# A fused attention and feed-forward kernel: attention tiles placed by a table, no warm-up matmuls, an order with a delay per unit, and another ending of the last block

## The chip, the cores and the metric

The kernel runs on one core of a Trainium2 chip. Time is device time in microseconds (us), the median of several executions. A profiled execution stands beside it: the trace has every instruction of the five engines (TensorE, called PE; VectorE, DVE; ScalarE, ACT; GpSimd, POOL; SyncE, SP), the DMA queues, and the clock granted to TensorE.

## The reference

Eight batches, eight heads, 576 tokens, head size 64, all in fp32. A random-feature attention comes first, then a feed-forward layer over all 4608 tokens:

```python
def phi(x):
    proj = np.einsum('bhsd,df->bhsf', x, w_phi)                  # 64 -> 128 features
    proj = proj - np.max(np.abs(proj), axis=-1, keepdims=True)
    return np.concatenate([np.exp(proj), np.exp(-proj)], axis=-1)
q_p, k_p = (phi(q), phi(k))
kv = np.einsum('bhsf,bhsd->bhfd', k_p, v);  z = np.sum(k_p, axis=2)
num = np.einsum('bhsf,bhfd->bhsd', q_p, kv)
den = np.einsum('bhsf,bhf->bhs', q_p, z)[..., None] + 1e-06
x = (num / den), heads side by side, (4608, 512)
h = x @ w_in                                                     # 512 -> 2048
out = (0.5 * h * (1 + erf(h / sqrt(2)))) @ w_out                 # 2048 -> 512
```

## The kernel before

**Attention**, batch by batch. `k_unit` projects 512 keys of two heads into a pair of PSUM banks (`pk`), VectorE takes the maximum of the absolute values and subtracts it, ScalarE makes the two exponentials (`ek`), and 80 small matmuls sum them with the values into `kv`. `q_front` projects queries (`pq`), ScalarE copies them out (`pc`), GpSimd takes the maximum over the partitions (`mb`), VectorE subtracts, ScalarE makes `ef`; then TensorE forms numerators (`pn`) and, in batches 0 to 2, denominators (`dn`). `xo` and `do` are the copies of these, which SP stores to DRAM. `quotients` fetches the denominators, takes reciprocals and stores them. Batch 0 has its queries in two halves; the other batches have a main part of 512 tokens and a rest of 64.

**Weights.** The inputs `w_in` and `w_out` come as 64-bit numbers. `split_weight` loads each of 32 pieces and makes a high and a low fp32r part of it, with five VectorE and two ScalarE instructions. A weight's tile (`w_i0_0` to `w_i3_3`, `w_o0` to `w_o15`) is empty until its raw load.

**The layer** runs over 18 blocks of 256 tokens. `tokens` fetches a block from DRAM, divides, and splits it into `xh` and `xl`. Each of 8 units in a block does two first-layer groups of 12 matmuls into a PSUM tile `ph` (`up`), a gelu on ScalarE, a split of its result, and the second-layer matmuls. Blocks 0 to 7 (`block`) sum in `po`. Blocks 8 to 17 (`seven`) use a seven-product scheme on 2x2 quarters: the products m1 to m7 are summed in `pa0`, `pa1` and `pb`, and at the block's end ScalarE copies four of them into two tiles `ob`, VectorE adds or subtracts the others, and the two tiles are stored. The sums of weights that this needs are made by `sums_of_weights` and kept in DRAM until block 8.

**What sets the order.** The program describes all operations to a planner (`Plan.op`), each with its engine, an assumed cost, the buffers that it reads and writes, and a rank. `Plan.order` then goes through a model of the engines: at each step the operation that can start first goes, and among those of an engine that can start together the lowest rank. A buffer has a tag with so many slots (`Plan.pool`); an operation that needs a slot waits in the model until one is free, and within a stream (`k`, `q`, `f`, `w`, ...) the buffers of a tag are taken in the order in which they were described. The order that comes out is emitted, and every engine's queue executes it strictly. TensorE leaves the layer's matmuls for attention work only if `LUMP` us of that work is ready or some of it has waited `LINGER` us. `PULL`, `URGE`, `BIAS` (for a change of ScalarE's table), `HOLD` (batch 1 not before), `WPACE` (a weight not before) and `SUMSAT`, `SUMSEACH` are further constants of the planner. Four matmuls on a tile of zeros (`WARM`, tile `spin`) open TensorE's queue.

`mm` is the helper at line 342 that issues every matmul, so that all matmuls have this line; `tt` (L383) and `copy` (L377) are the helpers of most VectorE and ScalarE instructions. L395 is the raw load of a weight, L475, L477 and L542 are the loads of keys, values and queries, L558 is the store of `xo`, L848 that of the last block.

Of the kernel before, what the change touches and what calls it, by code (L numbers as in the profile page):

```python
# [27 lines left out]
P = 128  # L28
# [13 lines left out]
class Buf:  # L42


    def __init__(self, plan, tag, make):
        self.plan, self.tag, self.make = plan, tag, make
# [12 lines left out]
class Op:  # L59
    __slots__ = ("eng", "cost", "fn", "bufs", "rank", "table", "late", "deps", "users", "wait", "ready", "start", "end", "n", "names", "nbytes", "duty", "kind", "port", "part", "reopen")  # L60


class Plan:
# [15 lines left out]
    def __init__(self, tc):  # L79
        self.banks = ("ph", "po", "pp", "kv", "pn")  # L80
        self.tc, self.ops, self.slots, self.lines, self.stream, self.since = tc, [], {}, {}, None, 0.0

# [188 lines left out]
def mm_cost(m, n):  # L271
    return n * 0.443 / 1e3
# [27 lines left out]
def fused_kernel(ctx: ExitStack, tc: tile.TileContext, qT, kT, va, w_st, w_in, w_out, out):  # L300
# [25 lines left out]
    def turn_over():  # L326
# [10 lines left out]
    ps = {t: plan.pool(ppool, t, n) for t, n in dict(ph=2, po=1).items()} | {  # L337
        t: plan.pool(lambda: shared[1], t, n) for t, n in dict(pp=1, kv=1, pn=1, pa0=1, pa1=1, h0=1, h1=1).items()}
    op = plan.op

# [48 lines left out]
    def split_weight(src, nm, rank):  # L389
        tag = f"w_{nm}"  # L390
        raw = plan.pool(spool, tag, 1)([P, 512, 2], U32, f"raw_{nm}")
# [63 lines left out]
    def k_rest(b, rank):  # L455
        k = lambda: dict(rank=next(rank))
        plan.stream = "k"
        kr = sb["kr"]([P, 2, P], F32, f"kr_{b}")
# [7 lines left out]
    def k_quad(b, g, kvs, rank, rest):  # L466
# [5 lines left out]
        kts, vts = [], []  # L472
        for p in range(2):
            kt = (early(4 * g + p) if b == 0 else sb["kt"])([P, 4 * P], F32, f"kt_{nm}_{p}")
            op("sp", 0.06, lambda kt=kt, p=p: nc.sync.dma_start(out=kt(), in_=kT[b, g, :, 4 * P * p : 4 * P * (p + 1)]), w=[kt], kb=262, **k())  # L475
# [3 lines left out]
            vts.append(vt)  # L479
        for p in range(2):  # L480
            kt, vt = kts[p], vts[p]
            e = [sb[EARLY_EK[p] if b == 0 else "ek"]([P, 2, 4, NF], F32, f"ek_{nm}_{p}_{s}") for s in (1, 0)][::-1]
# [50 lines left out]
    def q_pair(b, p, kvs, rank, halves=(0, 1)):  # L533
# [4 lines left out]
        for half in halves:  # L538
            nm = f"{b}_{p}_{half}"
            at, n = PIECES[b][half]  # L540
            main = "" if n == HS else " main"
# [45 lines left out]
    def q_rest(b, kvs, rank):  # L587
        k = lambda x=0: dict(rank=next(rank))
        plan.stream = "q"
        nm, n = f"{b}_rest", 4 * HR  # L590
# [46 lines left out]
    def quotients(b, half, rank):  # L637
        plan.stream = "r"
        nm = f"{b}_{half}"
# [30 lines left out]
    def tokens(j, rank):  # L670
        plan.stream = "f"
        xr = sb["xr"]([P, NCC, TB], F32, f"xr_{j}")
# [45 lines left out]
    def block(j, rank):  # L718
        x = tokens(j, rank)
        po = ps["po"]([P, 2, DM], F32, f"po_{j}")  # L720
        for u in range(NU):
            rk = rank(u / NU)
            ph = ps["ph"]([P, 2, TB], F32, f"ph_{j}_{u}")
            up(j, u, (2 * u, 2 * u + 1), ph, x, rk)
# [5 lines left out]
            for i in range(2):  # L730
# [12 lines left out]

                op("pe", 6 * mm_cost(128, DM), mm2, r=[gh, gl, wo[2 * u + i]], w=[po], rank=rk)
        for m in range(2):
            ob = sb["ob"]([P, DM], F32, f"ob_{j}_{m}")
# [6 lines left out]
    def sums_of_weights(rank):  # L753
# [3 lines left out]
        for k in range(NFC // 2):  # L757
# [3 lines left out]
            for i, (x, xc, y, yc, o) in enumerate((  # L761
                    (b, low_cols, a, high_cols, ALU.add), (b, low_cols, b, high_cols, ALU.add), (a, low_cols, a, high_cols, ALU.add),
                    (b, high_cols, a, high_cols, ALU.subtract), (a, low_cols, b, low_cols, ALU.subtract))):
                kw = dict(rank=rank(n / 40))
                plan.since = SUMSAT + SUMSEACH * n
                n += 1
# [10 lines left out]
    def fetch_sums(stored, rank, after):  # L777
        plan.stream = "t"
        tw = []
        for k in range(NFC // 2):  # L780
            kw = dict(rank=rank(k / 8) - 20)
            a, b, d = wo[k], wo[k + 8], stored[k]
            t = sb[f"tw{k}"]([P, 3, 2, HDM], F32R, f"tw_{k}")
# [6 lines left out]
    def seven(j, tw, rank, after):  # L790
# [4 lines left out]
        part = dict(m4=lambda: pa0()[:, left], m5=lambda: pa0()[:, right], m3=lambda: pa1()[:, left], m2=lambda: pa1()[:, right],  # L795
                    m7=lambda: pb()[:, 0, left], m6=lambda: pb()[:, 0, right], m1=lambda: pb()[:, 1, left])
        for u in range(NU):
            rk = rank(u / NU)
            ph = ph_all = ps["ph" if u % 4 < 2 else f"h{u % 2}"]([P, 2, TB], F32, f"ph_{j}_{u}")
            late = after if u < 4 else ()  # L800
            up(j, u, (u, u + 8), ph, x, rk, late if u > 1 else ())
            dr = dict(rank=URGE + rk)
# [22 lines left out]
                     ("m1", uh, ul, 2, lambda i, t=tw[u]: t()[:, 0, 1 - i]))  # L825
            for group, acc in ((terms[:2], pa0), (terms[2:4], pa1), (terms[4:6], pb), (terms[6:], pb)):

                def products(group=group, u=u):
                    ins = []
                    for m, h, l, n, w in group:  # L830
                        for g, i in ((h, 0), (h, 1), (l, 0)):
                            k = len(ins) % 3
                            ins.append(mm(part[m](), lhsT=g()[:, n], rhs=w(i), start=u == 0 and k == 0 and m in ("m4", "m3", "m7", "m1"),
                                          stop=u == NU - 1 and k == 2 and m in ("m5", "m2", "m6", "m1"), skip_group_check=True))
                    return ins

                op("pe", 3 * len(group) * mm_cost(128, HDM), products, r=[group[0][1], group[0][2], a, b, tw[u]], w=[acc], rank=rk)
# [3 lines left out]
        for c, m, x, acc in ((c11, 0, "m4", pa0), (c12, 0, "m5", pa0), (c21, 1, "m2", pa1), (c22, 1, "m3", pa1)):  # L841
            copy("act", act(HDM, True), c, part[x], [acc], [tops[m]], **kw)
        for c, m, x, acc, o in ((c11, 0, "m5", pa0, ALU.subtract), (c12, 0, "m3", pa1, ALU.add), (c21, 1, "m4", pa0, ALU.add), (c22, 1, "m2", pa1, ALU.subtract),
                                (c11, 0, "m7", pb, ALU.subtract), (c22, 1, "m6", pb, ALU.add), (c11, 0, "m1", pb, ALU.add), (c22, 1, "m1", pb, ALU.add)):
            tt("dve", dve(HDM, True), c, c, part[x], o, [acc, tops[m]], [tops[m]], port=False, **kw)
        for m in range(2):
            eng = "act" if j == NBLK - 1 and m else "sp"
            op(eng, 0.06, lambda m=m, eng=eng: (nc.scalar if eng == "act" else nc.sync).dma_start(  # L848
                out=out[j * TB + m * P : j * TB + (m + 1) * P, :], in_=tops[m]()), r=[tops[m]], kb=262, rank=rank(1))

# [32 lines left out]


SEVEN = 8
SUMS = 2
SUMSAT = 190.75
SUMSEACH = 4.989
SUMSPAN = 581.86
T15 = 870.02  # L890
T18 = 997.68
BIAS = 151.84
STICK = 2
PATIENCE = 4.09
URGE = -1000.0
EARLY = 41.32
WPACE = 4.81
# [11 lines left out]
HOLD = 32.35  # L909
WR = -23.78  # L910
# [3 lines left out]
POOLSLACK = 0.3  # L914
DMASLACK = 0.23
T0 = 85.1
# [43 lines left out]
```

## Time and profile before

| | |
|---|---|
| median of 3 runs | 1060.81 us (1060.12 to 1062.88) |
| profiled execution | 1061.28 us, span 1059.1 us |
| TensorE busy | 1028.1 us, 97% |
| VectorE busy | 680.2 us, 64% |
| ScalarE busy | 614.6 us, 58% |
| GpSimd busy | 276.6 us, 26% |
| mean granted clock of TensorE | 0.989 |

The span is from the first to the last instruction. Busy shares are means over stages that differ: attention and weights until about 200 us, the layer with attention in between until about 615 us, the layer alone after that. The ends of matmuls are modelled, so that a busy TensorE is not one at its peak; the steps between the starts of matmuls say more.

### The profile page before, as it was taken

Reading aid. Unit: us, or ns where it says so; the run is one execution under the profiler, and the core shown is the slowest. Engines: PE = TensorE matmul, PEld = TensorE weight load, DVE = VectorE, ACT = ScalarE, POOL = GpSimd, SP = SyncE. Lnnn points to the kernel's source line nnn. Section 1 sums busy time; section 2 is a strip of 40 time slices with the busy share of each in tenths; the row PEclk is TensorE's granted clock in tenths of the full one; section 3 lists DMA queues with packets and bytes.
Section 4 is the critical chain, followed back from the end, with each engine's and each line's share of the span. In section 5 each row is a group of like instructions: output and inputs, shape, how many; then the busy total and the mean of one; then the engine's idle time right before and its main releaser. Section 6 shows DMA issues by size and latency. Waiting matters only on the chain.

```text
span 1059.1 us, 24222 instructions
## 1 busy us (share of the span) xinstructions
PE 1028.1 (97%) x10083; PEld 897.7 (85%) x10083; DVE 680.2 (64%) x1209; ACT 614.6 (58%) x1007; POOL 276.6 (26%) x72
## 2 busy tenths in 40 slices
PE   6778999999999999999999999999999999999997
PEld 4555677778877778887887899999999999999997
DVE  4989999788797897256454333556465565565464
ACT  4878899778776668776465523334444344344343
POOL 2134221454255565565656310000000000000000
PEclk7989999999999999999999999999999999999999
DMA  7587672433535334124121166111111021021000
GB/s 263 153 256 220 198 224 77 132 126 123 153 119 160 104 125 149 56 75 127 34 75 42 60 235 224 41 41 41 41 41 41 21 61 37 24 61 29 14 21 20
DMA packets 87037, 107.10 MB, mean 101 GB/s; under 512 B 28988, under 2 KB 56700, under 8 KB 86928
## 3 DMA queue, kind: packets, MB, share of 16 engines
q1 hardware_dynamic: 86784, 105.30, 32.4%
q8 instruction: 79, 1.29, 0.5%
q14 instruction: 30, 0.25, 0.1%
q10 hardware_dynamic: 144, 0.26, 0.1%
HBM read 75.87 MB, written 29.66 MB: 100 GB/s over the span
## 4 chain that ended last, share of the span: by engine, by line
PE 83%; ACT 6%; DVE 6%; DMA 3%; issue 2%; SPq 0%; ACTq 0%; DVEq 0%
PE ph L342 34%; PE po L342 14%; PE pa L342 10%; PE pb L342 8%; PE kv L342 6%; PE pn L342 4%; PE pk L342 3%; PE pq L342 2%; DMA x_d<-xo 2%; DVE ts L383 1%; ACT ek L452 1%; ACT ef L524 1%; DMA t_d<-ts 1%; ACT L727 1%; DMA vt<-in_va_dram 1%
## 5 line engine op out<-in xcount | busy, mean ns | idle before, releaser
L342 PE MATMUL ph<-xh,w_i 128*128 128x256 f32 x2304 | 414.3, 278 | 0.0
L342 PEld LDWEIGHTS ph<-xh,w_i 128*128 128x128 f32 x2304 | 355.7, 188 | 8.9 <-issue 7.2
L342 PE MATMUL ph<-xl,w_i 128*128 128x256 f32 x1152 | 318.6, 277 | 0.0
L342 PEld LDWEIGHTS ph<-xl,w_i 128*128 128x128 f32 x1152 | 216.3, 188 | 0.2
L383 DVE TENSOR_TENSOR sg<-ga 128x256 f32<-128x256 f32 (+1 forms) x240 | 84.2, 376 | 155.3 <-ACT ga L804 147.7
L519 POOL PARTITION_ALL_REDUCE mb<-pc x36 | 122.2, 3395 | 169.4 <-ACT pc L377 138.4
L342 PE MATMUL po<-w_o,gh 128*128 128x512 f32 (+1 forms) x517 | 163.3, 398 | 0.0
L804 ACT ACTIVATE ga<-ph 128x512 f32<-128x512 f32 x80 | 48.0, 600 | 174.3 <-PE ph L342 172.5
L530 POOL PARTITION_ALL_REDUCE db<-pc x20 | 124.2, 6208 | 83.1 <-DVE pc L579 83.1
L342 PEld LDWEIGHTS po<-w_o,gh 128*128 128x128 f32 x517 | 93.2, 188 | 31.6 <-issue 5.2
L342 PE MATMUL pa<-w_o,oh 128*128 128x256 f32 x640 | 112.9, 276 | 0.0
L342 PE MATMUL po<-w_o,gl 128*128 128x512 f32 (+1 forms) x282 | 101.1, 373 | 1.2 <-DVE gl L383 1.2
L342 PEld LDWEIGHTS pa<-w_o,oh 128*128 128x128 f32 x640 | 96.4, 188 | 0.0
L383 DVE TENSOR_TENSOR gl<-ph,gh 128x512 fp32r<-128x512 f32 x64 | 44.0, 688 | 77.0 <-ACT ph L728 76.4
L342 PE MATMUL pa<-w_o,ol 128*128 128x256 f32 x320 | 88.3, 276 | 0.0
L342 PE MATMUL pb<-tw,uh 128*128 128x256 f32 x480 | 85.6, 276 | 0.0
L727 ACT ACTIVATE gh<-ph 128x512 fp32r<-128x512 f32 x64 | 38.3, 598 | 63.5 <-PE ph L342 63.0
L524 ACT ACTIVATE ef<-pc 128x1024 f32<-128x1024 f32 (+1 forms) x72 | 67.3, 972 | 11.1 <-DVE pc L383 10.9
L342 PEld LDWEIGHTS pb<-tw,uh 128*128 128x128 f32 x480 | 72.3, 188 | 0.0
L452 ACT ACTIVATE ek<-ek 128x1024 f32<-128x1024 f32 x64 | 67.6, 1058 | 6.9 <-DVE ek L383 6.2
L342 PE MATMUL kv<-vt,ek 128*64 128x65 f32 x2048 | 67.5, 225 | 0.0
L342 PE MATMUL pb<-tw,ul 128*128 128x256 f32 x240 | 66.3, 276 | 0.0
(90 smaller groups left out, 1596.2 us busy)
## 6 DMA issues: line engine op xcount, KB each, us to landing
vt<-in_va_dram SPq DMA_DIRECT2D x32, 325.0 KB
t_d<-ts SPq DMA_DIRECT2D x40, 256.0 KB
out_dram<-ob SPq DMA_DIRECT2D x35, 256.0 KB
kt<-in_kT_dram SPq DMA_DIRECT2D x32, 256.0 KB
raw_i<-in_w_in_dram SPq DMA_DIRECT2D x16, 512.0 KB
raw_o<-in_w_out_dram SPq DMA_DIRECT2D x16, 512.0 KB
qt<-in_qT_dram SPq DMA_DIRECT2D x28, 256.0 KB
x_d<-xo SPq DMA_DIRECT2D x28, 256.0 KB
```

What stands on the lines that cost most here:

```text
L342: return tc.keep_in_program_order(nc.tensor.matmul(*a, **kw))
L383: op(eng, cost, lambda: e.tensor_tensor(out=dst(), in0=a(), in1=b(), op=o), r=r, w=w, **kw)
L452: op("act", act(256 * n), lambda s=s: nc.scalar.activation(e[s](), e[1](), AF.Exp, scale=1.0 - 2.0 * s), r=[e[1]], w=[e[s]], table="exp", ...
L519: op("pool", plan.SPENT[most], lambda: nc.gpsimd.partition_all_reduce(mb(), pc(), P, bass_isa.ReduceOp.absmax), r=[pc], w=[mb], port=most, ...
L524: op("act", act(2 * n), lambda s=s: nc.scalar.activation(ef[s](), pc(), AF.Exp, scale=1.0 - 2.0 * s), r=[pc], w=[ef[s]], table="exp", **k())
L530: op("pool", plan.SPENT[total], lambda: nc.gpsimd.partition_all_reduce(db(), pc()[:, :2], P, bass_isa.ReduceOp.add), r=[pc], w=[db], port= ...
L727: op("act", act(2 * TB, True) + 0.016, lambda gh=gh, ph=ph: nc.scalar.activation(gh(), ph(), AF.Gelu), r=[ph], w=[gh], table="gelu", rank= ...
L804: op("act", act(2 * TB, True) + 0.037, lambda ph=ph, ga=ga: nc.scalar.activation(ga(), ph(), AF.Gelu), r=[ph_all], w=[ga], table="gelu", a ...
```

## The change

1. `Plan.pool` looks a tile's name up in a table `HOME`. Where it stands there, the tile takes a slot of the tag that the table gives and not of its own. The table has 210 tiles of batches 0 to 2: SBUF tiles go to the weights' tiles (`w_i0_2` to `w_i3_3`, `w_o8` to `w_o15`) or to other tags' slots (`xh`, `xl`, `gh`, `gl`, `ef`, `ek`, `pc`, `mb`, `db`); PSUM tiles go from `pp`, `kv` and `pn` to `po`, `ph` and each other.
2. `WARM` is 0: the four matmuls on zeros are gone.
3. Every operation belongs to a unit (`plan.unit`: a weight, half a pair of heads, a unit of a block, ...), and a table `DELAY` adds a number of its own to the ranks of each of 360 units. Constants of the planner change: `BIAS` 151.84 to 551.516, `PATIENCE` 4.09 to 2.138, `LUMP` 2.69 to 82.289, `LINGER` 4.65 to 6.494, `HOLD` 32.35 to 23.07, `WPACE` 4.81 to 4.989, `SUMSAT` 190.75 to 175.933, `SUMSEACH` 4.989 to 3.384, `DMASLACK` 0.23 to 0.517.
4. In the last block the product m6 has a bank of its own (`pc`, in the slot of `h1`); the first-layer groups rank 2.2 units earlier and use three slots; the products m1, m7 and m6 of the last two units come after all others, in this order; dependencies are kept by product and by quarter of the output and not by bank and tile; and the four quarters are stored one by one, 128 KB each, from SP's and ScalarE's queues in turn.

```diff
     def pool(self, pool, tag, bufs):
         self.slots[tag] = bufs
-        return lambda shape, dt, name: Buf(self, tag, lambda: (pool() if callable(pool) else pool).tile(shape, dt, tag=tag, name=name, bufs=bufs))
+        self.pools[tag] = pool
+        def new(shape, dt, name):
+            home = HOME.get(name, tag)
+            def make():
+                pool = self.pools[home]
+                return (pool() if callable(pool) else pool).tile(shape, dt, tag=home, name=name, bufs=self.slots[home])
+            b = Buf(self, home, make, name)
+            return b
...
+        o.unit = self.unit
+        o.rank += DELAY.get(self.unit, 0.0)
...
+        last = j == NBLK - 1
+        if last:
+            pc = ps["h1"]([P, DM], F32, f"pc_{j}")
+            part["m6"] = lambda: pc()[:, left]
...
-            up(j, u, (u, u + 8), ph, x, rk, late if u > 1 else ())
+            up(j, u, (u, u + 8), ph, x, rank((u - 2.2) / NU) if last else rk, late if u > 1 else ())
...
+            groups = [(u, terms[:2]), (u, terms[2:4])]
+            if last and u >= NU - 2:
+                put_off += [(x, u, terms[x : x + 1]) for x in (4, 5, 6)]
+            else:
+                groups += [(u, terms[4:6]), (u, terms[6:])]
+            if u == NU - 1:
+                groups += [(v, group) for x in (6, 4, 5) for y, v, group in put_off if x == y]
...
+        final = ((c11, 0, 0, "m7", ALU.subtract), (c22, 1, 1, "m6", ALU.add)), ((c11, 0, 0, "m1", ALU.add), (c22, 1, 1, "m1", ALU.add))
...
+        if last:
+            for m, h, eng in ((0, 1, "sp"), (1, 0, "act"), (0, 0, "sp"), (1, 1, "act")):
+                op(eng, 0.06, lambda m=m, h=h, eng=eng: (nc.scalar if eng == "act" else nc.sync).dma_start(
+                    out=out[j * TB + m * P : j * TB + (m + 1) * P, h * HDM : (h + 1) * HDM], in_=tops[m]()[:, h * HDM : (h + 1) * HDM]),
+                   r=[halves[m, h]], also=[tops[m]], kb=131, rank=rank(1))
+            return
...
+DELAY = {
+    "start": -1266.9, "k0r": -1919.4, "k00": -1383.5, "k01": -1239, "k02": -1008.7, "k03": -1069.9, "q000": -1527.1, "q010": -1691.4, "q020": -1252.1,
...
+HOME = {
+    "kr_0": "w_i2_3", "pk_0_r": "po", "mx_0_r": "gl", "er_0_1": "w_o10", "er_0_0": "xl", "kt_0_0_0": "ef", "vt_0_0_0": "w_i1_2", "kt_0_0_1": "xh",
...
-WARM = 4
+WARM = 0
...
-LUMP = 2.69
-LINGER = 4.65
+LUMP = 82.289
+LINGER = 6.494
```

## Rows read from the trace of the kernel before

**Rows 1.** The page: the span, and each engine's busy time, share and instructions.

```profile
span 1059.1 us, 24222 instructions
PE 1028.1 (97%) x10083; PEld 897.7 (85%) x10083; DVE 680.2 (64%) x1209; ACT 614.6 (58%) x1007; POOL 276.6 (26%) x72
```

**Rows 2.** Stretches: length, busy time of PE, PEld, DVE, ACT, POOL, granted clock, DMA.

```profile
0.00:40.00 40.00, 30.62 (x454) 23.08 (x454) 26.34 (x38) 22.68 (x35) 6.80 (x7) 0.83 0.63 217
40.00:80.00 40.00, 29.98 (x484) 21.03 (x488) 34.38 (x49) 30.31 (x56) 15.10 (x6) 0.91 0.81 229
...
360.00:400.00 40.00, 37.70 (x332) 29.98 (x332) 36.67 (x54) 27.00 (x42) 21.18 (x6) 1.00 0.38 122
...
680.00:720.00 40.00, 40.00 (x355) 40.00 (x354) 24.50 (x64) 17.60 (x39) 0.00 (x0) 1.00 0.13 41
```

**Rows 3.** The same view, the first 10 and 90 us and the 70 us after.

```profile
0.00:10.00 10.00, 6.66 (x16) 2.68 (x16) 0.48 (x1) 2.42 (x4) 1.24 (x5) 1.00 0.78 248
...
0.00:90.00 90.00, 67.88 (x1034) 47.37 (x1036) 70.68 (x97) 61.49 (x102) 25.75 (x14) 0.89 0.71 221
90.00:160.00 70.00, 69.64 (x830) 49.61 (x827) 63.92 (x102) 62.52 (x91) 22.61 (x7) 1.00 0.71 213
```

**Rows 4.** Timeline of the start: start, us, engine, line, operation, tiles, count [idle before].

```profile
1.17 0.89 SPq L542 DMA_DIRECT2D qt<-in_qT_dram  x2
...
2.27 5.22 PE L342 MATMUL spin<-idle 128*128 128x512 f32 x8 [2.27 <-ACT idle L364]
...
7.41 0.76 PE L342 MATMUL pq<-qt,wst 64*128 64x288 f32 x4
...
18.46 1.33 PE L342 MATMUL pq<-qt,wst 64*128 64x288 f32 x4 [1.46 <-issue]
```

**Rows 5.** Chain of waits until 120 us: start, us, what.

```profile
41.15 4.64 DMA x_d<-xo
...
58.19 4.41 DMA x_d<-xo
```

**Rows 6.** Waits from 20 to 80 us: us in total, times, longest.

```profile
PE pk L342 <- ACT pc L377: 5.2, 5, 1.5
ACT xo L377 <- DMA x_d<-xo: 3.1, 3, 1.4
```

**Rows 7.** Waits of SP's queue from 20 to 80 us.

```profile
SPq L558 <- ACT xo L377: 12.6, 4, 10.0
```

**Rows 8.** Timeline of the end, and one stretch of it.

```profile
1053.47 0.28 PE L342 MATMUL pb<-tw,ul 128*128 128x256 f32 x1
...
1054.77 1.20 DVE L383 TENSOR_TENSOR ob<-ob,pb 128x256 f32<-128x256 f32 x3
...
1056.00 0.37 ACTq L848 DMA_DIRECT2D out_dram<-ob  x1
...
1057.00:1058.00 1.00, 0.00 (x0) 0.00 (x0) 0.00 (x0) 0.00 (x0) 0.00 (x0) 0.50 0.59 221
```

**Rows 9.** Timeline of weight loads at the start, and the stretch from 13 to 25 us.

```profile
4.13 0.34 PEld L342 LDWEIGHTS spin<-idle 128*128 128x128 f32 x1 [0.52 <-issue]
...
6.03 0.19 PEld L342 LDWEIGHTS spin<-idle 128*128 128x128 f32 x1 [0.24 <-issue]
...
13.00:25.00 12.00, 9.59 (x98) 8.31 (x100) 9.74 (x12) 8.41 (x12) 4.16 (x2) 0.50 0.65 239
```

**Rows 10.** Timeline of TensorE around the first and the last change to attention work.

```profile
94.04 0.28 PE L342 MATMUL ph<-xh,w_i 128*128 128x256 f32 x1
94.25 1.94 PE L342 MATMUL pn<-ef,kvn 128*64 128x512 f32 x8
...
613.51 0.28 PE L342 MATMUL ph<-xl,w_i 128*128 128x256 f32 x1
613.62 0.28 PE L342 MATMUL ph<-xh,w_i 128*128 128x256 f32 x1
613.83 1.15 PE L342 MATMUL pn_rest<-ef_rest,kvn 128*64 128x64 f32 x32
```

More of the change, by code (lines that the diff above doesn't have):

```diff
@@ L59 @@
 class Op:
-    __slots__ = ("eng", "cost", "fn", "bufs", "rank", "table", "late", "deps", "users", "wait", "ready", "start", "end", "n", "names", "nbytes", "duty", "kind", "port", "part", "reopen")
+    __slots__ = ("eng", "cost", "fn", "bufs", "rank", "table", "late", "deps", "users", "wait", "ready", "start", "end", "n", "names", "nbytes", "duty", "kind", "port", "part", "reopen", "unit")
 class Plan:
@@ L80, in __init__ @@
         self.banks = ("ph", "po", "pp", "kv", "pn")
-        self.tc, self.ops, self.slots, self.lines, self.stream, self.since = tc, [], {}, {}, None, 0.0
+        self.pools = {}
+        self.tc, self.ops, self.slots, self.lines, self.stream, self.since, self.unit = tc, [], {}, {}, None, 0.0, "start"
     def turn(self, a, b):
@@ L338, in fused_kernel @@
         t: plan.pool(lambda: shared[1], t, n) for t, n in dict(pp=1, kv=1, pn=1, pa0=1, pa1=1, h0=1, h1=1).items()}
+    for tag in [f"w_o{f}" for f in range(NFC)] + [f"w_i{c}_{q}" for c in range(NCC) for q in range(4)]:
+        plan.pool(spool, tag, 1)
     op = plan.op
@@ L389, in split_weight @@
     def split_weight(src, nm, rank):
-        tag = f"w_{nm}"
+        tag = plan.unit = f"w_{nm}"
         raw = plan.pool(spool, tag, 1)([P, 512, 2], U32, f"raw_{nm}")
@@ L456, in k_rest @@
         k = lambda: dict(rank=next(rank))
-        plan.stream = "k"
+        plan.stream, plan.unit = "k", f"k{b}r"
         kr = sb["kr"]([P, 2, P], F32, f"kr_{b}")
@@ L473, in k_quad @@
         for p in range(2):
+            plan.unit = f"k{b}{2 * g + p}"
             kt = (early(4 * g + p) if b == 0 else sb["kt"])([P, 4 * P], F32, f"kt_{nm}_{p}")
@@ L480, in k_quad @@
         for p in range(2):
+            plan.unit = f"k{b}{2 * g + p}"
             kt, vt = kts[p], vts[p]
@@ L539, in q_pair @@
             nm = f"{b}_{p}_{half}"
+            plan.unit = f"q{b}{p}{half}"
             at, n = PIECES[b][half]
@@ L588, in q_rest @@
         k = lambda x=0: dict(rank=next(rank))
-        plan.stream = "q"
+        plan.stream, plan.unit = "q", f"q{b}r"
         nm, n = f"{b}_rest", 4 * HR
@@ L637, in quotients @@
     def quotients(b, half, rank):
-        plan.stream = "r"
+        plan.stream, plan.unit = "r", f"r{b}{half}"
         nm = f"{b}_{half}"
@@ L670, in tokens @@
     def tokens(j, rank):
-        plan.stream = "f"
+        plan.stream, plan.unit = "f", f"t{j}"
         xr = sb["xr"]([P, NCC, TB], F32, f"xr_{j}")
@@ L722, in block @@
             rk = rank(u / NU)
+            plan.unit = f"b{j}_{u}"
             ph = ps["ph"]([P, 2, TB], F32, f"ph_{j}_{u}")
@@ L744, in block @@
                 op("pe", 6 * mm_cost(128, DM), mm2, r=[gh, gl, wo[2 * u + i]], w=[po], rank=rk)
+        plan.unit = f"o{j}"
         for m in range(2):
@@ L764, in sums_of_weights @@
                 kw = dict(rank=rank(n / 40))
+                plan.unit = f"s{n}"
                 plan.since = SUMSAT + SUMSEACH * n
@@ L781, in fetch_sums @@
             kw = dict(rank=rank(k / 8) - 20)
+            plan.unit = f"f{k}"
             a, b, d = wo[k], wo[k + 8], stored[k]
@@ L796, in seven @@
                     m7=lambda: pb()[:, 0, left], m6=lambda: pb()[:, 0, right], m1=lambda: pb()[:, 1, left])
+        last = j == NBLK - 1
+        if last:
+            pc = ps["h1"]([P, DM], F32, f"pc_{j}")
+            part["m6"] = lambda: pc()[:, left]
+        own = {m: Buf(plan, None, None) for m in part}
+        held = dict(m4=pa0, m5=pa0, m3=pa1, m2=pa1, m7=pb, m6=pc if last else pb, m1=pb)
+        put_off = []
+        firsts = ("m4", "m3", "m7", "m1", *(("m6",) if last else ()))
+        stops = ("m5", "m2", "m6", "m1", *(("m7",) if last else ()))
         for u in range(NU):
             rk = rank(u / NU)
-            ph = ph_all = ps["ph" if u % 4 < 2 else f"h{u % 2}"]([P, 2, TB], F32, f"ph_{j}_{u}")
+            plan.unit = f"b{j}_{u}"
+            ph = ph_all = ps[("ph", "ph", "h0")[u % 3] if last else "ph" if u % 4 < 2 else f"h{u % 2}"]([P, 2, TB], F32, f"ph_{j}_{u}")
             late = after if u < 4 else ()
-            up(j, u, (u, u + 8), ph, x, rk, late if u > 1 else ())
+            up(j, u, (u, u + 8), ph, x, rank((u - 2.2) / NU) if last else rk, late if u > 1 else ())
             dr = dict(rank=URGE + rk)
@@ L825, in seven, with products @@
                      ("m1", uh, ul, 2, lambda i, t=tw[u]: t()[:, 0, 1 - i]))
[L826 to L828 removed]
+            groups = [(u, terms[:2]), (u, terms[2:4])]
[5 more added lines that the diff above has]
+                groups += [(v, group) for x in (6, 4, 5) for y, v, group in put_off if x == y]
+            for v, group in groups:
+                def products(group=group, u=v):
                     ins = []
@@ L832, in products @@
                             k = len(ins) % 3
-                            ins.append(mm(part[m](), lhsT=g()[:, n], rhs=w(i), start=u == 0 and k == 0 and m in ("m4", "m3", "m7", "m1"),
-                                          stop=u == NU - 1 and k == 2 and m in ("m5", "m2", "m6", "m1"), skip_group_check=True))
-                    return ins
-                op("pe", 3 * len(group) * mm_cost(128, HDM), products, r=[group[0][1], group[0][2], a, b, tw[u]], w=[acc], rank=rk)
+                            ins.append(mm(part[m](), lhsT=g()[:, n], rhs=w(i), start=u == 0 and k == 0 and m in firsts,
+                                          stop=u == NU - 1 and k == 2 and m in stops, skip_group_check=True))
+                    return ins
+                op("pe", 3 * len(group) * mm_cost(128, HDM), products, r=[group[0][1], group[0][2], wo[v], wo[v + 8], tw[v]],
+                   w=[own[m] for m, *_ in group], also=[held[m] for m, *_ in group], rank=rk)
+        plan.unit = f"o{j}"
         tops = [sb["ob"]([P, DM], F32, f"ob_{j}_{m}") for m in range(2)]
@@ L840, in seven @@
         kw = dict(rank=URGE + rank(1))
[L841 to L845, printed above, removed]
+        halves = {(m, h): Buf(plan, None, None) for m in range(2) for h in range(2)}
@@ new lines, in seven @@
+        for c, m, h, x in ((c11, 0, 0, "m4"), (c12, 0, 1, "m5"), (c21, 1, 0, "m2"), (c22, 1, 1, "m3")):
+            copy("act", act(HDM, True), c, part[x], [own[x]], [halves[m, h]], also=[tops[m], held[x]], **kw)
+        final = ((c11, 0, 0, "m7", ALU.subtract), (c22, 1, 1, "m6", ALU.add)), ((c11, 0, 0, "m1", ALU.add), (c22, 1, 1, "m1", ALU.add))
+        for c, m, h, x, o in ((c11, 0, 0, "m5", ALU.subtract), (c12, 0, 1, "m3", ALU.add), (c21, 1, 0, "m4", ALU.add), (c22, 1, 1, "m2", ALU.subtract),
+                              *final[last], *final[not last]):
+            tt("dve", dve(HDM, True), c, c, part[x], o, [own[x], halves[m, h]], [halves[m, h]], also=[tops[m], held[x]], port=False, **kw)
```

27 lines of the change are left out of this document (15 added, 12 removed), and 69 rows, old and new, of tables (DELAY, HOME).

## The prediction

> **What bounds the kernel now.** I read the busy shares first: TensorE is at 97% of a span of 1059.1 us [rows 1], so only what TensorE does not do in the other 3%, does slowly, or does between two kinds of work can be won. The stretches of 40 us then say where that lies [rows 2]. From 680 us on a stretch is 40.00 of 40 us busy with 355 matmuls, at clock 1.00: nothing to win there except at the very end. In the first two stretches TensorE is busy 30.62 and 29.98 us at a granted clock of 0.83 and 0.91; 360 to 400 us has 2.30 us idle. Over the first 90 us it is 67.88 of 90 busy [rows 3], so 22.1 us are idle, 2.3 of them before the first matmul [rows 4].
>
> What ends the waits there: the chain of waits runs four times through the store of an attention result, `x_d<-xo`, from 41.15 us on; first and last of the four pieces take 4.64 and 4.41 us [rows 5]. ScalarE cannot write the next `xo` until one of its two tiles has been stored. ScalarE itself stands only 3.1 us for it, and TensorE waits 5.2 us, five times, for ScalarE to clear the one bank pair that projections use (`pk` after `pc`) [rows 6]. So the start is a net of few buffers, in which TensorE, ScalarE and SP take turns.
>
> The engine behind it is VectorE: 70.68 of the first 90 us, and 63.92 of the next 70 [rows 3], which is 91%. Once TensorE is full it is VectorE (splitting weights, the attention's maxima and differences) that decides how early the layer can be fed.
>
> The profiled execution took 1061.28 us, 2.2 us more than its span; the median of the runs is 1060.81. I sum against 1061.28 and take off the 0.5 at the end.
>
> **The change part by part.**
>
> *Tiles of batches 0 to 2 by the table.* No instruction is added or removed; the same tiles lie elsewhere, so that `xo`, `do`, `pc`, `ef`, `ek` no longer queue for two tiles of their own, and projections, `kv`, `pn` and `dn` get the layer's `ph` and `po` banks. That removes the store from the chain [rows 5] and most of the 5.2 us [rows 6]. What is late next is VectorE. It cannot start before a projection: its first 10 us hold 0.48 us of work now [rows 3]. Between 10 and 160 us it works 134 of 150 us (70.68 + 63.92 less that start) [rows 3], so the whole slack behind the start is 16 us; it has to do the same work before TensorE can be fed. Upper bound of the gain 16 us, lower bound 0 (VectorE as slack as today). Below nothing is the rival at the end. In 90 to 160 us, with no such queue, VectorE stands at 91%; bringing 10 to 90 us from 70.2/80 = 88% to about 96% shortens that stretch to 73 us. I take 7 us.
>
> The table adds waits too: a weight's raw load cannot be issued until the attention tile that lies in its place has been read. SP is one queue in program order, and behind a waiting load stand all other loads and stores; SP already waits up to 10.0 us in one piece for an `xo` to be written [rows 7]. I take this as hidden by loads issued well ahead; its price without that cover is the last rival.
>
> *No matmuls on zeros.* Four warm-up matmuls (8 passes in the trace) fill TensorE from 2.27 us for 5.22 us, and the first projection follows on their heels at 7.41 [rows 4]. Its input is issued from 1.17 us on [rows 4]. How long such a load takes is not in a row; the nearest is the last store, 3.1 us from issue to the end of the span [rows 8], so the projection could start near 4.5 us: 3 us earlier at best, 0 if the load lands at 7. Against that stands the clock. [...] Net I take 0.5 us gained, bounds 3 gained and 1.7 lost, outside the clock rival below.
>
> [...]
>
> *Order by a delay per unit, and the planner's constants.* All instructions stay; their order on TensorE, ScalarE, VectorE and SP changes over the whole run. Two things can be priced. First, the limits on leaving the layer's matmuls: the planner now waits until a piece of attention work has stood 6.494 us (4.65 before), and no longer until 2.69 us of it are there. Each excursion costs a turn: within a run the step is 0.11 us, into the attention work 0.21 (94.04 to 94.25, and at the last 613.62 to 613.83) [rows 10]. That is 0.1 us more; for the way back I take the same, an estimate, so 0.2 per excursion. I count 63 of them between 94 and 615 us, of which the first and the last stand in the rows: 12.6 us in all. If their number falls as 4.65 to 6.494, to 45, 18 turns go: 3.6 us; I take 3.5. Bounds 0 and 12.6. Second, the idle time of 360 to 400 us [rows 2]: 2.30 us. I take 1 us off, bounds 2.3 gained and 2.3 lost (an order that makes as large a hole elsewhere). The larger cost of a table switch on ScalarE and the earlier sums of weights I put at nothing: they only matter where VectorE and ScalarE are full, which is in the 7 us above; after 400 us TensorE has no idle time that they could fill.
>
> *Last block's ending.* The first-layer matmuls of the last block come 2.2 units earlier, and products m1, m7, m6 of the last two units are put behind the others; the same matmuls at the same step, no DMA moved. Their cover is TensorE's own full queue (40.00 of 40) [rows 2]; without it a gelu chain of some 2 us would show. After the last matmul (ends 1053.47 + 0.28 = 1053.75) VectorE now works until 1055.97, and the second store is issued at 1056.00; the end is 1059.1 [rows 8]: 5.35 us. Afterwards one difference is left: a third of 1.20, 0.40 us, behind some 0.3 us of hand-over, then the store: 0.7 instead of 2.25, 1.5 saved. The store is half as large; data still moved for 0.59 of the microsecond from 1057 [rows 8], so 0.3 of that may go too. I take 1.8, bounds 1.2 and 2.4.
>
> Sum: 7 + 0.5 + 3.5 + 1 + 1.8 = 13.8 us; 1061.3 - 13.8 - 0.5 = **1047**.
>
> **The rivals.**
>
> *VectorE holds the start where it is.* For it: 91% from 90 to 160 us with TensorE full. Against it: 88% before, with waits for `pk` and stores in between. Then 7 us fall away: 1054.
>
> [...]
>
> *Everything priced comes in:* 16 at the start, 2.4 at the end, 5 of turns, 2.3 of holes, 2 from the zeros: 27.7, so 1033. Against it: VectorE would have to work without a gap for 150 us.
>
> *Slower: weights late behind attention tiles.* Place: SP's queue from 60 to 150 us, where the raw loads of the late weights now wait for tiles of batches 1 and 2 to be read. The first layer block cannot finish until every weight is split, and only one block sums at a time, so TensorE falls back on attention work alone, at the rate of the first 80 us: 60.6 of 80 [rows 2], 24% idle. Over 70 us that is 17 us, against which stand the 6.8 us of the other parts: 1061.3 + 17 - 6.8 - 0.5 = 1071. It decides the sign from about 7 us of new idle time. For it: one wait of 10.0 us on SP already [rows 7]. Against it: loads of weights are far fewer than the time for them, and the table covers mostly late weights.
>
> **How the numbers follow.** Forecast 1047: 0.57 (its own range 1040 to 1052). VectorE holds: 0.17. Clock: 0.06. Everything: 0.07. Slower: 0.13. The range 1036 to 1059 leaves out part of the best case and the slower one. A measurement of this kernel tells about 0.3% from no change: 1057.6 to 1064.0. Faster takes nearly all of the first four, 0.80; within takes the edge of "VectorE holds" and a weak form of the slower case, 0.09; slower 0.11.
>
> **What would show it.** Right: no `x_d<-xo` in the chain before 90 us; TensorE's idle time in the first 90 us at about 15 in place of 22 us, VectorE there above 76; fewer than 50 excursions; 3.5 us from the last matmul to the end, with one VectorE instruction between. [...] Slower rival: TensorE below 95% between 80 and 200 us. The prediction is wrong if VectorE's share before 160 us does not rise, or if holes of several us appear after 200 us.

## The result, and the profile after

The changed kernel takes 1047.34 us (median of 4 runs, 1045.0 to 1049.29), the kernel before 1061.85 in the same runs; the ratio is 0.9859, with a 95% interval of 0.9825 to 0.9893. The prediction was 1047. Its total is right, and by place most of its terms come close; what stands behind them is in part something else, and the larger part of this section and the next is about that.

The page of the kernel after: span, busy times, and the shares of the chain of waits by engine.

```profile
span 1046.6 us, 24197 instructions
PE 1019.6 (97%) x10070; PEld 893.1 (85%) x10070; DVE 661.1 (63%) x1209; ACT 614.5 (59%) x1011; POOL 276.9 (26%) x72
PE 90%; DVE 5%; ACT 2%; issue 1%; DMA 1%; SPq 0%; DVEq 0%; ACTq 0%
```

Stretches of it (length, then busy time of PE, PEld, DVE, ACT, POOL, clock, DMA).

```profile
0.00:10.00 10.00, 3.62 (x28) 3.08 (x28) 2.59 (x4) 2.43 (x4) 0.19 (x4) 1.00 0.76 227
...
0.00:40.00 40.00, 27.34 (x504) 21.80 (x504) 29.12 (x38) 26.35 (x45) 9.12 (x8) 0.96 0.77 255
...
0.00:90.00 90.00, 70.38 (x1126) 49.62 (x1127) 72.66 (x98) 65.43 (x109) 30.19 (x15) 0.92 0.73 237
90.00:160.00 70.00, 68.25 (x789) 49.10 (x788) 67.56 (x104) 60.55 (x90) 22.71 (x7) 1.00 0.60 187
160.00:200.00 40.00, 38.73 (x540) 31.51 (x534) 38.39 (x63) 37.03 (x56) 8.07 (x3) 1.00 0.41 117
...
360.00:400.00 40.00, 40.00 (x331) 32.87 (x331) 27.44 (x44) 29.93 (x39) 19.33 (x4) 1.00 0.39 121
...
680.00:720.00 40.00, 40.00 (x355) 40.00 (x355) 19.01 (x54) 14.29 (x33) 0.00 (x0) 1.00 0.05 16
```

Beside [rows 2, 3]: in the first 90 us TensorE is busy 70.38 us in place of 67.88, of which 5.14 (7.41 - 2.27) were zeros [rows 4]: 62.74 us of the kernel's own work became 70.38. From 90 to 160 us it is 1.39 us less busy than before, from 360 to 400 the hole of 2.30 us is gone, and from 680 on nothing has changed. VectorE, on which the prediction built, is no denser between 10 and 90 us in this trace: 70.08 us where it was 70.20. It starts earlier, from 90 to 160 us it is denser (67.56 us in place of 63.92), and in the first 90 us it does other work. Its lines of the first 90 us that finish the split of a weight, first of the kernel before, then of the one after (line, operation, tiles, count, busy time and mean ns, idle time before):

```profile
L383 DVE TENSOR_TENSOR w_i<-wt_i,w_i 128x512 fp32r<-128x512 f32 x8 | 5.5, 687 | 0.2
L383 DVE TENSOR_TENSOR w_o<-wt_o,w_o 128x512 fp32r<-128x512 f32 x4 | 2.8, 710 | 1.9 <-ACT w_o L377 1.9
```

```profile
L401 DVE TENSOR_TENSOR w_i<-wt_i,w_i 128x512 fp32r<-128x512 f32 x6 | 4.0, 683 | 0.0
L401 DVE TENSOR_TENSOR w_o<-wt_o,w_o 128x512 fp32r<-128x512 f32 x4 | 2.7, 683 | 0.0
```

Ten weights are split in that time and not twelve; summed over its instructions VectorE spends 36.1 us on weights in place of 40.3, and 40.4 on attention in place of 32.4. A likely reason why that helps, which no run tests by itself: an attention instruction releases matmuls at once, a weight only when the rest of its column block is there.

The start and the chain of waits (first the timeline of TensorE, then pieces of the chain: start, us, what):

```profile
6.31 1.23 PE L360 MATMUL pk_r<-wst,kr 64*128 64x128 f32 x8 [6.31 <-DMA wst<-in_w_st_dram]
7.29 1.95 PE L360 MATMUL pk<-wst,kt 64*128 64x128 f32 x16
```

```profile
27.80 1.67 DMA x_d<-xo
...
55.61 5.54 DMA vt<-in_va_dram
...
70.56 3.48 DMA qt<-in_qT_dram
```

The store of `xo`, four times in the chain before [rows 5], is there once, with 1.67 us. What is late next are loads: values at 55.61, queries at 70.56. The waits of TensorE from 20 to 90 us (us in total, times, longest; the three longest are shown) no longer name `pk` behind `pc`, 5.2 us from 20 to 80 us before [rows 6], but single waits:

```profile
PE pq L360 <- DVE ek L401: 3.0, 1, 3.0
PE kv L360 <- DMA vt<-in_va_dram: 2.3, 1, 2.3
PE dn L360 <- ACT do L395: 2.2, 1, 2.2
```

The end, by the timelines of TensorE, VectorE and ScalarE:

```profile
1042.12 0.28 PE L360 MATMUL pc<-tw,ul 128*128 128x256 f32 x1
```

```profile
1040.73 1.69 DVE L401 TENSOR_TENSOR ob<-ob,pa 128x256 f32<-128x256 f32 x4 [1.87 <-ACT ob L395]
1042.34 1.08 DVE L401 TENSOR_TENSOR ob<-ob,pb 128x256 f32<-128x256 f32 x3
1043.33 0.41 DVE L401 TENSOR_TENSOR ob<-ob,pc 128x256 f32<-128x256 f32 x1
```

```profile
1040.05 1.05 ACT L395 COPY ob<-pa 128x256 f32<-128x256 f32 x3 [1.79 <-PE pa L360]
1041.59 0.37 ACT L395 COPY ob<-pa 128x256 f32<-128x256 f32 x1 [0.49 <-DVE ob L401]
```

The last matmul ends at 1042.40, VectorE at 1043.74, the span at 1046.64: 1.34 us of VectorE and 2.90 of store, 4.24 us in all. Before it was 2.23 and 3.16, 5.39 us [rows 8].

The two spans differ by 12.5 us. By place, from the starts and busy times of the two traces:

| | before | after | gained |
|---|---|---|---|
| until the first attention matmul | 7.41 | 6.31 | 1.1 |
| TensorE idle from there to 90 us | 19.85 | 13.30 | 6.55 |
| idle 90 to 200 us | 0.74 | 3.03 | -2.3 |
| idle 320 to 400 us | 2.76 | 0.00 | 2.75 |
| idle 400 us to the last matmul | 0.00 | 0.15 | -0.15 |
| TensorE busy without the zeros (clock, turns) | 1022.98 | 1019.61 | 3.4 |
| after the last matmul | 5.39 | 4.24 | 1.15 |

These are two single executions. A second trace of the changed kernel (below) has 11.66 us in the second row in place of 13.30 and 1020.76 in the sixth in place of 1019.61, so the rows on the start and on busy time are good to about 2 us only.

### The profile page after: what moved, and what is told of

The parts are those of the page before. It is cut to its first block, busy times and chain, and to the rows that moved or that the text cites. A ratio compares the mean times of both kernels' runs of the same rounds, so it can differ in the third digit from the quotient of the medians.

```text
span 1046.6 us, 24197 instructions
## 1 busy us (share of the span) xinstructions
PE 1019.6 (97%) x10070; PEld 893.1 (85%) x10070; DVE 661.1 (63%) x1209; ACT 614.5 (59%) x1011; POOL 276.9 (26%) x72
## 4 chain that ended last, share of the span: by engine, by line
PE 90%; DVE 5%; ACT 2%; issue 1%; DMA 1%; SPq 0%; DVEq 0%; ACTq 0%
PE ph L360 38%; PE po L360 17%; PE pa L360 10%; PE pb L360 7%; PE kv L360 6%; PE pn L360 4%; PE pk L360 3%; PE pq L360 3%; PE dn L360 1%; DVE wt_i L421 1%; PE pn_rest L360 1%; DMA vt<-in_va_dram 1%; DVE ek L401 0%; DVE wt_i L423 0%; DVE pc L401 0%
## 5 line engine op out<-in xcount | busy, mean ns | idle before, releaser
L401 DVE TENSOR_TENSOR ul<-sg,uh 128x384 fp32r<-128x384 f32 x80 | 44.6, 558 | 71.5 <-ACT uh L395 70.3
L360 PE MATMUL pb<-tw,uh 128*128 128x256 f32 x464 | 82.9, 276 | 0.1
L395 ACT CAST uh<-sg 128x384 fp32r<-128x384 f32 x80 | 41.0, 512 | 50.6 <-PE pb L360 25.3
L360 PEld LDWEIGHTS pb<-tw,uh 128*128 128x128 f32 x464 | 69.9, 188 | 0.3 <-DVE ob L401 0.3
L360 PE MATMUL pn<-ef,kvn 128*64 128x512 f32 (+1 forms) x288 | 64.9, 571 | 1.9 <-ACT do L395 0.8
```

What stands on the lines that cost most here:

```text
L360: return tc.keep_in_program_order(nc.tensor.matmul(*a, **kw))
L395: op(eng, cost, lambda: nc.scalar.copy(out=dst(), in_=src()), r=r, w=w, **kw)
L401: op(eng, cost, lambda: e.tensor_tensor(out=dst(), in0=a(), in1=b(), op=o), r=r, w=w, **kw)
```

## The experiments

Where "the same order" is said, the instructions of every engine stand as in the kernel from which the experiment starts, but for the edit itself. Otherwise the planner orders anew.

**The zeros, each way.** Both keep the order.

```diff
+    plan.done = [o for o in plan.done if o.rank != -5000.0]   # before, without the four matmuls
```

```diff
+    # after: four matmuls on `idle` into a tile of tag "pn", issued ahead of TensorE's first operation
```

> The kernel before, the same order on every engine, only the four warm-up matmuls on zeros left out. Prediction's step: 0.5 us gained (bounds 3 gained, 1.7 lost): the first projection starts at 4.5 to 6.5 us in place of 7.41, and later waits take most of it back, so 1059.5 to 1061. [...]

> The changed kernel, the same order, with the four matmuls on zeros put back at the head of TensorE's queue. If the zeros cost what the step says, 0 to 1.5 us slower than the changed kernel (first projection at about 7.4 in place of 6.31 us). [...]

Without zeros the kernel before takes 1059.26 us against 1061.13 (ratio 0.9981, 0.9967 to 0.9994): 1.9 us. The trace of this run is of its fastest execution (1055.28 us), so only the start is read from it. The changed kernel with zeros takes 1048.76 (ratio to the kernel before 0.9886, 0.9865 to 0.9906); without them it was 0.9859 and, run again, 0.9886 (below), so no difference is shown there. TensorE's first rows, first before without zeros, then after with them:

```profile
3.51 1.33 PE L342 MATMUL pq<-qt,wst 64*128 64x288 f32 x4 [3.51 <-DMA qt<-in_qT_dram]
5.57 1.33 PE L342 MATMUL pq<-qt,wst 64*128 64x288 f32 x4 [0.73 <-ACT pc L377]
```

```profile
2.27 5.47 PE L363 MATMUL spin<-idle 128*128 128x512 f32 x8 [2.27 <-ACT idle L385]
7.67 0.71 PE L363 MATMUL pk_r<-wst,kr 64*128 64x128 f32 x8
8.26 1.16 PE L363 MATMUL pk<-wst,kt 64*128 64x128 f32 x16
```

The first projection starts 3.9 us earlier (3.51 against 7.41) and takes 1.33 us in place of 0.76, as long as the one at 18.46 us in the kernel before, where the granted clock was 0.50 [rows 4, 9]. In the order after, the zeros cost 1.36 us of start (7.67 against 6.31) and give most of it back: 0.71 in place of 1.23 us and 1.16 in place of 1.95. So in the kernel before the zeros stand in the way of a load that has landed; in the order after, the next projections are shorter with the zeros, but a gain in time from them is shown nowhere. That the granted clock stays low longer after the change, to which the prediction gives a chance of 0.06, did not come true: nothing became slower, the changed kernel's granted clock over the first 40 us is 0.96 in place of 0.83 [rows 2] (its records begin at 9.3 us, those of the kernel before at 5.4), and the stretch at 0.50 that lasted from 12.2 to 25.8 us before lasts from 12.7 to 16.1; in all, 13.7 us at 0.50 are on record until the last matmul in place of 20.5.

**The ending, each way.** First the kernel before with the new ending (its ranks, places, constants and zeros kept), then the changed kernel with the old one.

```diff
-DELAY = {...}; HOME = {...}; new constants
+DELAY = {}; HOME = {}; constants of before
```

```diff
-        last = j == NBLK - 1
+        last = False
```

> The kernel before (its ranks, constants, places and zeros) with the new ending of the last block and its finer dependencies alone. Step: 1.8 us gained; by the tail seen in the changed kernel (4.24 us after the last matmul in place of 5.39) 1.2 us. So 1058.5 to 1060, a tail near 4.2 us, and nothing else different. Rival: the earlier first-layer groups starve the second layer and TensorE idles in the last block, 2 us or more back.

> The changed kernel with the old ending of the last block; its order is the same up to that block. If the ending is worth its tail, 1.2 us slower than the changed kernel. Rival: the delays of the last block's units fit the new ending only, TensorE gets idle time in the last block, and it is 4 us or more slower.

The ending alone: 1059.97 against 1061.13 us, ratio 0.9989 (0.9976 to 1.0002), with 4.25 us after the last matmul in place of 5.39. The size is as these say, 1.2 us; the interval just reaches no change. The changed kernel with the old ending: 1050.32, ratio 0.9892 (0.9869 to 0.9915); the interval overlaps that of the changed kernel, so its time alone decides nothing. Its trace, of its slowest execution (1053.4 us), has 1.51 us of idle time for TensorE after 400 us (0.15 with the new ending), so here the delays do fit the new ending better, as the rival says, by about 1.4 us. The granted clock fell there as well:

```profile
1040.00:1046.00 6.00, 4.63 (x26) 4.10 (x25) 3.36 (x9) 3.27 (x8) 0.00 (x0) 0.79 0.00 1
```

Its tail, the time from the end of the last matmul to the end of the span, is 4.89 us and not 5.39, so in the changed kernel the old ending's tail costs 0.65 us more than the new one's.

**Places of `xo` and `do` alone, each way,** at a fixed order: the changed kernel with these tiles in two slots again, and the kernel before with them, for batches 0 and 1, in the tiles of `w_i0_3` to `w_i3_3` in turn.

```diff
-                pool = self.pools[home]
+                pool = self.pools[tag if name[:3] in ("xo_", "do_") else home]
```

```diff
+PUT = {"xo_0_0_0": "w_i0_3", "do_0_0_0": "w_i1_3", "xo_0_1_0": "w_i2_3", ...}
```

> The changed kernel, the same order on every engine, but the copies xo and do of batches 0 to 2 back in their two own slots. If places of xo and do carry the gain at the start, the store of xo is in the chain again and TensorE's idle time before 90 us rises by 3 us or more. Rival (the order carries it, the store was only what the chain happened to go through): under 1 us.

> The kernel before, the same order on every engine, but the copies xo and do of batches 0 and 1 (main parts) in the tiles of four late weights in turn. If the waits for the store bind, ScalarE's 3.1 us of waits go and the time falls by 2 to 4 us. Rival (order binds): under 1 us either way, and the waits turn up under another name.

The first takes 1051.17 us, ratio 0.9918 (0.989 to 0.9947): 3 to 4 us above the changed kernel by medians, with overlapping intervals. TensorE's idle time from its first matmul to 90 us, which was to rise by 3 us or more, is 13.92 us; the changed kernel's two traces have 13.30 and 11.66. Its chain has the store again three times:

```profile
26.45 1.67 DMA x_d<-xo
44.27 5.98 DMA x_d<-xo
...
64.54 4.06 DMA x_d<-xo
```

The second gains nothing: ratio 0.9994 (0.998 to 1.0009), although ScalarE waits for no store any more before it writes an `xo` (3.1 us before [rows 6]). In the chain of waits the store is still there:

```profile
41.26 4.13 DMA x_d<-xo
46.35 3.89 DMA x_d<-xo
```

So the rival holds for the kernel before: in an order that was made for two slots, more slots are worth nothing. That an order made for more slots needs them is not shown, neither by the time nor by the idle time.

The chain is a weak witness here, because it is the path of one execution. In the kernel before without zeros, in the same order, it goes through the store of `xo` once before 90 us (at 54.64), and in the kernel before with the new ending, where VectorE and ScalarE work in the same order until 600 us, not at all; [rows 5] are from a trace in which it did so four times. TensorE's idle time from its first own matmul (one not on zeros) to 90 us is nearly the same in the three: 19.70, 18.87 and 19.85 us.

**Table without delays, and delays without table.** The planner finds no order for the whole table at the old ranks; for the entries of batches 0 and 1 it does. Both runs start from the changed kernel and keep its new ending. The first has the zeros and the old constants, the second neither, so that "delays" means here the delays with the new constants.

```diff
-DELAY = {...}; HOME = {...}; new constants
+DELAY = {}; HOME = {tiles of batches 0 and 1}; constants of before
```

```diff
-HOME = {...}
+HOME = {}
```

> The kernel before with the new ending and the table for batches 0 and 1, without delays and with the old constants: the planner orders anew. The prediction's step gives the table 7 us by itself: 1052 to 1055. Rival (the table only pays with an order made for it): no gain or slower than the kernel before, TensorE's idle time before 90 us no smaller than 22 us.

> The changed kernel with its delays and constants but without the table of places: the planner orders anew. If the order by delays carries the gain alone, within 3 us of the changed kernel. If table and delays only work together, slower than the kernel before, TensorE idle before 160 us by 30 us or more.

Table without delays: 1065.47 against 1061.97 us, ratio 1.0038 (1.0024 to 1.0053), slower. Delays without table: 1082.08, ratio 1.0207 (1.0178 to 1.0236), slower still. Their stretches, first of the table alone, then of the delays alone:

```profile
0.00:90.00 90.00, 73.97 (x1158) 48.56 (x1160) 75.03 (x100) 67.31 (x111) 31.83 (x16) 0.94 0.74 240
90.00:160.00 70.00, 63.59 (x692) 46.43 (x690) 66.88 (x110) 53.48 (x82) 10.85 (x5) 0.98 0.61 181
160.00:200.00 40.00, 38.39 (x413) 28.58 (x409) 32.39 (x43) 32.53 (x49) 9.40 (x3) 1.00 0.39 110
```

```profile
0.00:90.00 90.00, 66.48 (x987) 49.46 (x988) 67.39 (x97) 60.64 (x99) 22.07 (x13) 0.92 0.65 211
90.00:160.00 70.00, 63.78 (x615) 42.33 (x615) 64.86 (x90) 55.94 (x83) 29.14 (x8) 0.95 0.67 204
```

The table without delays does bring the start: idle time between the first attention matmul and 90 us falls from 19.85 to 13.77 us, about what the changed kernel has (13.30 and 11.66). With the delays without the table it is 18.93. But from 90 to 160 us TensorE has 6.4 us idle where it had 0.36 [rows 3], from 160 to 200 another 1.6, and 5.3 after 200 us (2.8 before), and the gain is given back. It is not the weights that come late, as the slower rival had it: the last raw load of a weight is issued at 149.9 us there, at 151.0 before, and after the real change at 162.5; the last weight is split at 181.0, 183.9 and 192.6 us. TensorE's longest wait from 90 to 200 us in the run with the table, 3.7 of its 8.0 us of idle time there, is that of a projection `pq` for VectorE's last reading of a `pk`. No data pass between the two, so it is for a PSUM bank that projections share:

```profile
PE pq L360 <- DVE ek L401: 3.7, 1, 3.7
```

For the delays without the table this is not settled: its longest wait of TensorE there, 4.6 us before a `pq`, names nothing that released it.

The traces also answer whether the start is set by how busy VectorE is (us; idle time from the first own matmul to 90 us):

| trace | VectorE busy, 10 to 90 us | TensorE idle |
|---|---|---|
| kernel before | 70.20 | 19.85 |
| kernel before, new ending | 69.88 | 18.87 |
| changed kernel | 70.08 | 13.30 |
| changed kernel again | 70.12 | 11.66 |
| changed kernel, three units put off (below) | 73.94 | 12.64 |
| table without delays | 74.24 | 13.77 |

It is not: TensorE's idle time is short with VectorE as busy as before and with VectorE busier. What goes with it is the work that VectorE does first. Every trace with 11 to 14 us of idle time has 39 to 41 attention instructions of VectorE before 90 us, every trace with 18 to 21 us has 31 to 36. Whether that is the cause or the effect no run separates.

**The limits on leaving the layer, alone.** The kernel before with two constants.

```diff
-LUMP = 2.69
-LINGER = 4.65
+LUMP = 82.289
+LINGER = 6.494
```

> The kernel before with LUMP and LINGER of the change alone; the planner orders anew. By the prediction's step the excursions fall from 63 towards 45 and 3.5 us are gained, with no new holes: 1057. Rival (holding attention work back starves what hangs on it): excursions fall, but TensorE gets idle time, above all before 200 us, and the kernel is slower than before.

1078.25 against 1061.29 us, ratio 1.0162 (1.0139 to 1.0185). Excursions: 62 in place of 63.

```profile
0.00:90.00 90.00, 68.50 (x1054) 46.52 (x1056) 69.31 (x98) 63.35 (x105) 27.50 (x15) 0.92 0.70 223
90.00:160.00 70.00, 66.57 (x700) 47.87 (x702) 66.17 (x101) 55.54 (x84) 15.08 (x5) 1.00 0.63 192
160.00:200.00 40.00, 36.42 (x337) 26.99 (x333) 32.73 (x47) 30.27 (x45) 9.43 (x3) 0.96 0.37 109
```

TensorE idles 3.4 us from 90 to 160 and 3.6 from 160 to 200 us, before 0.36 and 0.38; after 200 us it is 6.05 in place of 2.76. Of the 14.9 us by which this trace's span is longer, idle time after 90 us makes up 9.6; 5.0 are longer busy time of TensorE, which has 23.9 us at a granted clock of 0.50 on record in place of 20.5. As a price for the two constants by themselves the step of the prediction is wrong in count and in sign, and the rival is right about the idle time and the sign. The other constants were not tried by themselves.

**What sets the tail.** The changed kernel again for comparison, then with the products of three units or of one put off.

```diff
-            if last and u >= NU - 2:
+            if last and u >= NU - 3:     # uh and ul of unit 5 in the tile xr
```

```diff
-            if last and u >= NU - 2:
+            if last and u >= NU - 1:
```

> The changed kernel again, as the measure for the others of this call and for the runs with zeros, with the old ending and with two slots: 1046 to 1049 us.

> The changed kernel with the products m1, m7 and m6 of the last three units put off in place of two, the extra operands in the tile xr, which is free by then; the order before the last block is the same. If VectorE's eight operations in a row, which start when pa0 and pa1 are complete, set the tail, they start 1 us earlier against the last matmul: the tail falls from 4.24 to about 3.5 us. If the tail is the last matmul, one difference and the store, as predicted, it stays at 4.2.

> The changed kernel with the products of the last unit alone put off. If VectorE's row of operations sets the tail, it grows by the 1 us of matmuls that no longer lie behind pa0 and pa1: about 5.2 us. By the prediction's account it stays at 4.2.

Again: 1048.09 us, ratio 0.9886 (0.9867 to 0.9906). Three: 1046.34, 0.9861 (0.9841 to 0.9882). One: 1047.86, 0.9879 (0.986 to 0.9898). A difference in time between the three is not shown; the tails are 4.25, 4.22 and 4.92 us. The last matmuls end at 1040.20 (three) and 1041.06 (one). VectorE, first with three, then with one put off:

```profile
1038.51 1.69 DVE L401 TENSOR_TENSOR ob<-ob,pa 128x256 f32<-128x256 f32 x4 [1.97 <-ACT ob L395]
1040.12 1.07 DVE L401 TENSOR_TENSOR ob<-ob,pb 128x256 f32<-128x256 f32 x3
1041.11 0.41 DVE L401 TENSOR_TENSOR ob<-ob,pc 128x256 f32<-128x256 f32 x1
```

```profile
1040.08 1.68 DVE L401 TENSOR_TENSOR ob<-ob,pa 128x256 f32<-128x256 f32 x4 [2.56 <-ACT ob L395]
1041.68 1.07 DVE L401 TENSOR_TENSOR ob<-ob,pb 128x256 f32<-128x256 f32 x3
1042.67 0.41 DVE L401 TENSOR_TENSOR ob<-ob,pc 128x256 f32<-128x256 f32 x1
```

In all of them the eight operations stand in one row of 3.0 us from the start of the first; the row begins 1.69, 1.67 and 0.98 us before the last matmul ends, with three, two and one unit put off. From two to one this moves the tail by 0.68 us, as the row says. From two to three nothing moves: the last `pa` products wait for the last gelu, what is put off and ready goes ahead of them meanwhile, and in both cases 15 matmuls are left behind them. So my expectation for three fails for a reason of order. No version was shown to be faster than the changed kernel.

## Why the prediction was right or wrong, point by point

**Tiles by the table, 7 us: right in size at the start, wrong in mechanism, and no gain without the delays.** The idle time until 90 us fell by 6.55 us, and the wait of `pk` for `pc` from 20 us on, 5.2 us before, is gone. The prediction put that to the table by itself, to the store that leaves the chain, and to a denser VectorE, "88% to about 96%". The table without delays does shorten the start, but the kernel becomes 0.38% slower, because it gives the gain back after 90 us. The store in the chain was the path of one execution; two other traces of the same order go through it once and not at all, with as much idle time. And the density of VectorE does not go with the idle time: in the trace after it stayed at 70.08 of 80 us, 88%, with 8.0 us more on attention and 4.2 less on weights; in the run with the table it was 93%. In the runs here the gain belongs to the table and the delays (with their constants) together. That the best delays for no table, or the best table for the old ranks, would not do better was not tried: each alone was tested with the other's partner missing.

**No matmuls on zeros, 0.5 us: too small in the kernel before (1.9 us), not resolved in the kernel after.** The interval of the 1.9 us is 0.6 to 3.5, and the 1.9 lies within the bounds of the step, 3 gained and 1.7 lost. The bound "near 4.5 us" for the first projection was too late: it starts at 3.51 when its load alone holds it. No run shows the 0.5 us that stands in the sum, nor 1.7 us as what the zeros can be worth; the runs show in their place 1.9 us gained without the zeros, with the first two projections at 1.33 us each in place of 0.76, 1.14 us together.

**Turns, 3.5 us: wrong in count, near in size by luck.** Excursions fell from 63 to 57, not 45; at 0.2 us each that is 1.2 us. Their number does not follow the limit in proportion: with the two constants alone it is 62, and that kernel is 17 us slower. That the delays keep this cost away in the changed kernel is likely and not shown, since no run has the table and the delays with the old limits. TensorE's busy time without zeros is 3.4 us lower after. The clock explains little of the other 2.2: on record TensorE worked 16.5 us at a granted clock of 0.50 before and 13.2 after, and after come 2.9 us ahead of the first record, where `pk_r` and `pk` took 1.23 and 1.95 us in place of 0.71 and 1.16 with zeros. If half of that time is lost, an estimate from the granted clock of 0.50, half of 16.5 and half of 16.1 differ by 0.2 us. What the other 2 us are stays open.

**Idle time of 360 to 400 us, 1 us: 0.3 in all, by cancellation.** The hole is gone (2.30, and 0.46 from 320 to 360), and 90 to 200 us has 2.3 us more than before, 400 us to the end 0.15.

**The ending, 1.8 us: mis-sized, 1.15.** The last store, of half the size, took 0.26 us less, about as assumed (0.3). The step that failed is "afterwards one difference is left": four were left, because the first four of the eight cannot start before ScalarE's copies of `pa0` and `pa1`, and these start only 2.35 us before the last matmul ends (1040.05, 1042.40). VectorE ends 1.34 us after the last matmul, not 0.7.

**The sum** of 13.8 us stood against 12.85 by the profiled executions (1061.28 to 1048.43), 14.5 by the medians. By place it was 7.5 us for the start (7.65 measured, the first two rows of the table), 3.5 for TensorE's own work (3.4), 1 for holes (0.3) and 1.8 for the ending (1.15). That the first two agree so well is partly luck: the start came by another mechanism than the one that was priced, and of the 3.4 us the priced cause, fewer turns, explains 1.2.

**The rivals.** "VectorE holds the start where it is" did not come true: VectorE was as busy from 10 to 90 us as before, and TensorE's idle time fell all the same. A full engine can feed another sooner if it does other work first; that this is the reason here is likely and not shown. The slower rival happened in the two halves of the change, at 90 to 200 us where it was put; with the table alone through a shared projection bank and smaller holes, not through late weights.

**The signs named in advance.** Wrong: VectorE above 76 us in the first 90 (72.66), fewer than 50 excursions (57), 3.5 us of tail with one VectorE instruction (4.24, four); the idle time of 22 to 15 us counts the zeros as work and came to 19.6. Right but for one piece: no `x_d<-xo` in the chain. None of the signs of being wrong appeared: VectorE's busy time before 160 us did rise, from 134.6 to 140.2 us (84% to 88%), only not between 10 and 90 us; TensorE is 95.6% busy from 80 to 200 us, 97.1% before, just above the 95% named for the slower rival; after 200 us it idles 0.15 us in all. So these signs could not tell the mechanism that was priced from the one that came.

## What to carry to other kernels

Where a static order and a placement are searched together, neither has a price of its own: predict them as one, from the idle time of the engine that bounds, stage by stage, and look in the stages behind for what is given back. A second engine at 90% did not fix the start here; look at which of its work comes first, and not only at how full it is. A chain of waits is the path of one execution; before a cost is put on a piece of it, see whether a second trace of the same order goes the same way. For a tail, count the whole row of dependent operations from the event that releases its first, not only the operation behind the last matmul.

## What was not expected of the hardware

The four matmuls on zeros cost 1.9 us in the kernel before, although the first two projections take 0.57 us less each behind them (0.76 in place of 1.33): without the zeros the loads of the first projection have landed by 3.51 us, earlier than the zeros make way for it (7.41). With the last store at 128 in place of 256 KB, the time from VectorE's last result to the end is only 0.26 us shorter, 2.90 in place of 3.16 us. Eight of nine traces with the new ending show 2.90, the ninth 3.20; the old ending shows 3.15 to 3.44.
